# Thirteen FFN evictions, three result copies and two casts of v move from VectorE to ScalarE, and the PSUM banks are dealt out anew

## The chip, the core and the metric

The kernel runs on one core of a Trainium2 chip. The core has five engines, each with its own instruction queue, worked off strictly in order: TensorE (PE) multiplies matrices into PSUM, VectorE (DVE) and ScalarE (ACT) read PSUM and SBUF, GpSimd (POOL) works on SBUF, and SyncE (SP) issues DMAs. The engines wait for each other through semaphores. PSUM has eight banks of 128 partitions by 512 float32 values. The metric is the device time of one execution in microseconds (us), the lower the better. The three runs of the kernel before gave 174.99, 175.62 and 176.35 us, a median of 175.62.

## The reference

Windowed attention with a few global positions, and behind it a feed-forward network (FFN) with a maximum over three products:

```python
scores = scale * np.matmul(q, k.transpose(0, 1, 3, 2))        # 4 batches, 8 heads, 768 x 768, 64 wide
is_global = pos[None, :] < 8
is_local = (rel >= 0) & (rel < 96)
scores = scores + bias                                        # -slope of the head * distance
scores = np.where(is_global | is_local, scores, -1e9)
a = exp(scores - max) / sum
attn = np.matmul(a, v)                                        # to x: 3072 tokens x 512
h = np.maximum(np.maximum(x @ w1, x @ w2), x @ w3)            # 3072 x 768
out = h @ w_out                                               # 3072 x 512, float32
```

## The kernel before

The 3072 tokens are 24 tiles T of 128 (six for each batch). A tile's attention needs its own keys and those of the tile before it, since a query sees 96 positions back, with the 8 global positions copied into rows of the tile before. The FFN takes the tiles in seven chunks c of 4, 2, 2, 4, 4, 4 and 4 tiles (`SIZES`), so a product of a chunk has 512 columns, or 256 in chunks 1 and 2.

The whole order of work is written out by hand in the string `SCHEDULE`. Each word is a unit: a letter, numbers, and behind `@` the slot that the unit's output takes. The order of the words is the order in every engine's queue, and the slot decides who has to wait for whom: a unit that writes a slot waits until all readers of what lay there before are done. The units that matter here:

- `F c.f.j @bank`: PE, four matmuls of input product j (0, 1, 2) of FFN block f (0 to 5) of chunk c into a PSUM bank (line 433).
- `f c.f.j.how @slot`: the eviction of that product. For j = 0 it is a copy into the bf16 buffer h01, by ScalarE if `how` is 0 and by VectorE if it is 1 (line 447). For j = 1 VectorE takes the maximum with h01 in place (line 449), and for j = 2 the maximum into the buffer ht (line 452). There are five h01 slots.
- `O c.tt @bank`: PE, six matmuls of the second product of one tile (line 457); `o c.tt.how @slot` copies its result to SBUF, by ScalarE (0) or VectorE (1) (line 471); `s` issues its DMA to memory from SP (line 477).
- `v T.e.how`: casts half of a v tile to bf16, by ScalarE (0), VectorE (1) or GpSimd (2) (line 254).
- `S`, `e`, `m`, `A`, `n` of a tile: the scores (PE, two banks, line 349), the exponential (ACT, line 356), the mask (DVE, lines 365 and 367), the product with v (PE, two banks, lines 391 and 394), and the reciprocal and division (DVE, lines 402 and 403).
- `t` and `u`, or `Z`: the transposition of the attention's result to xT by PE and a copy, or by a DMA of SP (line 424). `x`, `y`, or `X`: the same for q and k. `l` loads q, k and v, `c` casts q and k (line 195, or 201 on GpSimd).
- `E`: the second product of all four tiles of the last chunk, the last of them in three pieces, with their copies and stores (lines 457, 462 and 463); its banks come from `LAST_BANKS`. One product of chunk 5, `O5.0`, is left behind it.

The index `how` picks the engine in one line:

```python
copies = (nc.scalar.copy, nc.vector.tensor_copy, nc.gpsimd.tensor_copy)
```

Of the kernel before, what the change touches and what calls it, by code (L numbers as in the profile page):

```python
# [611 lines left out]
```

## Time and profile before

| what | value |
|---|---|
| median of three runs | 175.62 us (174.99 to 176.35) |
| the profiled execution's own time | 176.69 us |
| its span, first to last instruction | 174.8 us |
| TensorE busy | 165.9 us, 95% |
| VectorE busy | 131.9 us, 75% |
| ScalarE busy | 95.4 us, 55% |
| GpSimd busy | 54.7 us, 31% |
| granted TensorE clock | 0.996 of full speed |

The profile is one execution on the chip. Busy times of PE are modelled at the ends, since matmuls are pipelined: a 512-column matmul is shown with 0.379 us, while the next one starts 0.216 us after it. So PE's share says little by itself; what it loses is seen in gaps between the starts of matmuls and in the idle time that is written behind a row in brackets, with what ended it. A row of a group reads: line, engine, operation, output<-input, shapes, count, then busy us and mean ns of one, then idle us before these instructions and what ended it. A few records of matmuls are missing.

### The profile page before, as it was taken

To read this page: it belongs to the slowest core of one execution; us is meant where nothing else is said; L and a number is where in the kernel's file an instruction comes from. 1 tells how busy PE (TensorE), PEld (TensorE's weight loads), DVE (VectorE), ACT (ScalarE), POOL (GpSimd) and SP (SyncE) were. 2 spreads that over 40 slices of the span, in tenths; PEclk is the share of its full clock that TensorE was granted. 3 is DMA by queue.
4 is the path that set the end of the run, shared out by engine and by line. 5 is a ranking of instruction groups with operands and counts; after the bars stand their busy time and mean duration, and the time that the engine had idled before them with its cause. 6 is when DMAs were issued, how large, how long until landed. Compare 5 with 4: busy or idle time off the path is not lost.

```text
span 174.8 us, 3865 instructions
## 1 busy us (share of the span) xinstructions
PE 165.9 (95%) x1485; PEld 93.6 (54%) x1507; DVE 131.9 (75%) x268; ACT 95.4 (55%) x147; POOL 54.7 (31%) x99
## 2 busy tenths in 40 slices
PE   7997999999999999898999999999999999999991
PEld 2555745577676877544445545544445554444460
DVE  7889864988599897989898678899578993074910
ACT  5988897672868788440667688200345651402051
POOL 4049295057586717003730003240530000000000
PEclk9999999999999999999999999999999999999998
DMA  5999999999899899999996759998990046370035
GB/s 149 352 292 327 402 360 385 270 371 311 229 303 179 139 183 266 267 290 284 165 135 112 114 145 306 305 210 260 231 213 20 0 120 137 121 286 4 0 119 185
DMA packets 66403, 37.36 MB, mean 214 GB/s; under 512 B 24144, under 2 KB 61392, under 8 KB 66384
## 3 DMA queue, kind: packets, MB, share of 16 engines
q1 hardware_dynamic: 66240, 37.04, 83.3%
q8 instruction: 12, 0.20, 0.5%
q10 hardware_dynamic: 144, 0.07, 0.1%
q14 instruction: 7, 0.06, 0.1%
HBM read 25.17 MB, written 6.29 MB: 180 GB/s over the span
## 4 chain that ended last, share of the span: by engine, by line
PE 76%; DVE 10%; DMA 6%; ACT 3%; issue 2%; SPq 0%; DVEq 0%
PE psum L433 44%; PE psum L457 17%; PE psum L349 6%; DMA xT<-xb 3%; DMA rawqk<-in_k_dram 3%; DVE P L365 3%; PE psum L391 3%; PE psum L394 2%; PE psum L276 2%; DVE ht L452 1%; DVE xb L403 1%; ACT P L356 1%; PE psum L270 1%; DVE qb L195 1%; PE psum L335 1%
## 5 line engine op out<-in xcount | busy, mean ns | idle before, releaser
L433 PE MATMUL psum<-xT,w 128*128 128x512 bf16 (+1 forms) x491 | 97.5, 348 | 1.5 <-DMA xT<-xb 0.7
L433 PEld LDWEIGHTS <-w 128*128 128x128 bf16 x504 | 47.6, 98 | 42.9 <-DMA xT<-xb 0.9
L356 ACT ACTIVATE P<-psum 128x1024 bf16<-128x1024 f32 (+1 forms) x48 | 43.3, 954 | 10.4 <-PE psum L349 10.3
L449 DVE TENSOR_TENSOR h<-h,psum 128x512 bf16<-128x512 bf16 (+1 forms) x42 | 25.0, 605 | 15.9 <-PE psum L433 12.4
L457 PE MATMUL psum<-wo,ht 128*128 128x512 bf16 (+2 forms) x147 | 33.4, 362 | 0.5
L447 ACT CAST h<-psum 128x512 bf16<-128x512 f32 (+1 forms) x27 | 13.8, 523 | 33.1 <-PE psum L433 29.8
L452 DVE TENSOR_TENSOR ht<-h,psum 128x512 bf16<-128x512 bf16 (+1 forms) x42 | 26.2, 644 | 2.1 <-PE psum L433 0.9
L365 DVE TENSOR_TENSOR P<-P,wmask 128x1024 bf16<-128x1024 bf16 x34 | 25.2, 752 | 2.0 <-ACT P L356 1.7
L457 PEld LDWEIGHTS <-ht 128*128 128x128 bf16 x156 | 13.8, 98 | 13.5 <-DVE ht L452 0.2
L254 POOL CAST va<-rawv 64x512 bf16<-64x512 f32 x28 | 18.5, 668 | 4.8 <-DMA rawv<-in_v_dram 3.7
L323 POOL COPY va<-vaf 4x260 int32<-4x260 int32 x17 | 7.2, 424 | 34.9 <-PE psum L394 34.5
L403 DVE TENSOR_TENSOR xb<-psum,rz 128x512 bf16<-128x512 f32 x24 | 16.6, 692 | 0.8
L201 POOL CAST qb<-rawk 128x512 bf16<-128x512 f32 x12 | 7.5, 654 | 23.7 <-DMA rawk<-in_k_dram 23.7
L349 PE MATMUL psum<-qkT 64*128 64x128 bf16 x352 | 14.4, 217 | 0.5 <-DVE qkT L315 0.4
L391 PEld LDWEIGHTS <-P 128*128 128x128 bf16 x192 | 12.6, 97 | 3.2 <-ACT P L356 0.4
L349 PEld LDWEIGHTS <-qkT 64*128 64x128 bf16 x352 | 10.0, 94 | 7.9 <-issue 5.9
L391 PE MATMUL psum<-va,P 128*128 128x65 bf16 x160 | 12.7, 193 | 0.7 <-DVE ht L452 0.6
L447 DVE CAST h<-psum 128x512 bf16<-128x512 f32 (+1 forms) x15 | 9.1, 615 | 5.1 <-PE psum L433 5.1
L471 ACT COPY staging<-psum 128x512 f32<-128x512 f32 x14 | 8.2, 592 | 8.8 <-PE psum L457 8.8
L201 POOL CAST qb<-rawq 128x512 bf16<-128x512 f32 x14 | 8.9, 664 | 9.0 <-DMA rawq<-in_q_dram 5.0
L394 PEld LDWEIGHTS <-P 128*128 128x128 bf16 x160 | 10.5, 97 | 2.1 <-issue 0.7
L394 PE MATMUL psum<-va,P 128*128 128x65 bf16 x128 | 9.9, 193 | 0.0
(72 smaller groups left out, 120.6 us busy)
## 6 DMA issues: line engine op xcount, KB each, us to landing
rawv<-in_v_dram SPq DMA_DIRECT2D x12, 512.0 KB, 7.0
out_dram<-staging SPq DMA_DIRECT2D x21, 256.0 KB, 2.7
rawq<-in_q_dram SPq DMA_DIRECT2D x10, 512.0 KB, 7.1
rawk<-in_k_dram SPq DMA_DIRECT2D x10, 512.0 KB, 7.3
staging<-in_moe_w_dram SPq DMA_DIRECT2D x3, 1024.0 KB, 9.3
staging<-in_moe_w_dram SPq DMA_DIRECT2D x3, 512.0 KB, 8.8
staging<-in_moe_w_out_dram SPq DMA_DIRECT2D x3, 512.0 KB, 6.3
out_dram<-staging SPq DMA_DIRECT2D x5, 128.0 KB, 2.2
```

The costliest lines, as they stand in the source:

```text
L254: copies[how](heads(va(T))[64 * e:64 * e + 64, :, 0:D], src)
L349: nc.tensor.matmul(sp[:, hh, j2, ds], qT(T - ds, 1, hsl, jp), qT(T, 0, hsl, jp), start=not how, stop=True, skip_group_check=True)
L356: nc.scalar.activation(P[:, :, 0:n], sps[T, g].rearrange("p a b d n -> p (a b) d n")[:, :, 0:n], AF.Exp, bias=0.0, scale=scale)
L365: mul(P, P, wmask[:, g, :, 0:2])
L391: nc.tensor.matmul(o, P[:, i, 0], heads(va(T))[:, h], start=True, stop=(t == 0), skip_group_check=True)
L394: nc.tensor.matmul(o, P[:, i, 1], heads(va(T - 1))[:, h], start=False, stop=True, skip_group_check=True)
L403: nc.vector.tensor_tensor(out=x.rearrange("p (g h) d -> p g h d", g=2), in0=o4[:, :, :, 0:64], in1=rz[:, :, :, None].to_broadcast([128, 2, ...
L433: nc.tensor.matmul(ps, w123[f // 2][:, j, dm, (f % 2) * 128:(f % 2) * 128 + 128], xT[c][:, dm], start=(dm == 0), stop=(dm == 3))
L447: copies[how](h01, ps)
L449: nc.vector.tensor_max(h01s[c, f], h01s[c, f], ps)
L452: nc.vector.tensor_max(dst, h01s[c, f].rearrange("p (t e i) -> p t e i", e=2, i=64), ps.rearrange("p (t e i) -> p t e i", e=2, i=64))
L457: nc.tensor.matmul(po, ht[c][:, f, tt * 128:(tt + 1) * 128], wo[:, f, cols], start=(f == 0), stop=(f == NF - 1))
```

## The change

Only the two strings of numbers change: the order of the units stays word for word. Eighteen units get another engine, VectorE (1) before and ScalarE (0) after:

- `f` with j = 0 of (chunk.block) 0.4, 1.2, 1.5, 2.5, 3.0, 3.1, 4.1, 4.0, 5.2, 5.1, 6.2, 6.4 and 6.5;
- `o` 0.1, 2.0 and 4.0;
- `v` 17.1 and 17.0.

ScalarE runs each at the place that the word has in the common order. Beside that, 99 units that write PSUM get other banks, nearly all of them `F`, `O`, `S`, `A` and `t`, and `LAST_BANKS` is dealt anew. The diff, cut to some of its lines:

```diff
-    e3.1@7 V2.1.2 n0@1 t0@2 W0.0.2 c1.2.2.1 u0.0@0 x2.1.2@3 y2.1.2.0@2 w1.2@2 x2.0.2@2 A3@4 t1@6 u1.0 n2@2
+    e3.1@7 V2.1.2 n0@1 t0@2 W0.0.2 c1.2.2.1 u0.0@0 x2.1.2@3 y2.1.2.0@2 w1.2@2 x2.0.2@4 A3@6 t1@2 u1.0 n2@2
...
-    F1.5.0@3 m7.0.1 v8.1.2 F1.5.1@4 A7@6 f1.5.0.1@0 m6.1.1 m6.0.1 o0.2.0@0 y4.1.2.0@0 f1.5.1.1 f1.5.2.1
-    x4.0.2@3 y4.0.2.0 G7.0 l0.6.2@1 c0.6.2.2 F1.4.2@5 O0.1@4 f1.4.2.1 n7@2 o0.1.1@1 A6@0 l2.5.2@2 S8.1.0@2
+    F1.5.0@3 m7.0.1 v8.1.2 F1.5.1@4 A7@6 f1.5.0.0@0 m6.1.1 m6.0.1 o0.2.0@0 y4.1.2.0@0 f1.5.1.1 f1.5.2.1
+    x4.0.2@3 y4.0.2.0 G7.0 l0.6.2@1 c0.6.2.2 F1.4.2@1 O0.1@2 f1.4.2.1 n7@2 o0.1.0@1 A6@0 l2.5.2@2 S8.1.0@4
...
-    F3.4.0@2 F3.0.0@1 f3.4.0.0@4 f3.0.0.1@0 m13.0.1 v13.1.1 f2.4.2.1 F3.1.0@4 F3.3.0@5 c0.9.2.0@2 f3.3.0.0@1
-    A12@2 n12@1 f2.3.2.1 f3.1.0.1@2 F3.1.1@1 f3.1.1.1 v13.0.1 l1.9.2@0 c1.9.2.1 F3.0.2@0 F3.0.1@5 f3.0.1.1
-    F3.1.2@4 f3.0.2.1@1 F3.2.0@1 F3.2.2@2 l1.7.2@6 c1.7.2.2 f3.1.2.1 F3.5.0@3 A13@4 V13.1.1 f3.5.0.1@3 n13@0
+    F3.4.0@2 F3.0.0@1 f3.4.0.0@4 f3.0.0.0@0 m13.0.1 v13.1.1 f2.4.2.1 F3.1.0@4 F3.3.0@1 c0.9.2.0@2 f3.3.0.0@1
+    A12@2 n12@1 f2.3.2.1 f3.1.0.0@2 F3.1.1@0 f3.1.1.1 v13.0.1 l1.9.2@0 c1.9.2.1 F3.0.2@1 F3.0.1@2 f3.0.1.1
+    F3.1.2@0 f3.0.2.1@1 F3.2.0@3 F3.2.2@2 l1.7.2@6 c1.7.2.2 f3.1.2.1 F3.5.0@0 A13@4 V13.1.1 f3.5.0.1@3 n13@0
...
-    V16.0.2 m19.0.1 l0.10.2@3 F4.0.1@0 F4.1.1@7 m19.1.1 f4.4.0.0@1 F4.5.2@6 c0.10.2.2@2 A19@2 Z16 n19@1 Z19
-    G19.0 s0.1 V19.0.2 s2.1 f4.1.1.1 f4.1.2.1@0 V19.1.1 F4.0.0@4 F4.4.1@5 A17@2 c1.10.2.0 f4.0.0.1@3 n17@2
-    F4.5.1@7 f4.5.1.1 F4.2.1@1 F4.3.2@4 f4.5.2.1 f4.4.1.1 F4.0.2@2 F4.3.1@3 F4.4.2@5 f4.2.1.1 v22.1.1
-    f4.0.1.1 f4.3.1.1 f4.0.2.1 f4.3.2.1 F4.2.2@1 Z17 F5.1.1@0 F5.2.0@3 F5.5.0@2 s1.1 F5.3.0@4 F5.0.0@6
+    V16.0.2 m19.0.1 l0.10.2@3 F4.0.1@0 F4.1.1@2 m19.1.1 f4.4.0.0@1 F4.5.2@3 c0.10.2.2@2 A19@4 Z16 n19@1 Z19
+    G19.0 s0.1 V19.0.2 s2.1 f4.1.1.1 f4.1.2.1@0 V19.1.1 F4.0.0@6 F4.4.1@7 A17@4 c1.10.2.0 f4.0.0.0@3 n17@2
+    F4.5.1@2 f4.5.1.1 F4.2.1@1 F4.3.2@6 f4.5.2.1 f4.4.1.1 F4.0.2@2 F4.3.1@3 F4.4.2@7 f4.2.1.1 v22.1.1
+    f4.0.1.1 f4.3.1.1 f4.0.2.1 f4.3.2.1 F4.2.2@0 Z17 F5.1.1@1 F5.2.0@6 F5.5.0@2 s1.1 F5.3.0@3 F5.0.0@4
...
-    F6.4.0@4 F6.2.0@7 f6.0.0.0@2 f6.0.1.1 F6.4.1@2 f6.0.2.1@0 F6.3.1@5 o4.2.0@6 f6.2.0.1@3 F6.3.0@3
-    f6.4.0.1@0 F6.1.1@4 f6.4.1.1 f6.4.2.1 s4.3 s4.0 f6.3.0.0@4 F6.3.2@1 F6.1.0@2 s5.2 F6.2.1@3 s4.2 s5.1
-    s4.1 f6.1.0.0@1 s3.0 s5.3.2 f6.3.1.1 f6.1.1.1 f6.3.2.1 f6.2.1.1 F6.2.2@2 f6.2.2.1 f6.1.2.1 F6.5.1@4
-    F6.5.0@1 f6.5.0.1@2 F6.5.2@5 f6.5.1.1 f6.5.2.1 E@7 O5.0@2 o5.0.0@5 s5.0.2
+    F6.4.0@2 F6.2.0@7 f6.0.0.0@2 f6.0.1.1 F6.4.1@3 f6.0.2.1@0 F6.3.1@5 o4.2.0@6 f6.2.0.0@3 F6.3.0@4
+    f6.4.0.0@0 F6.1.1@2 f6.4.1.1 f6.4.2.1 s4.3 s4.0 f6.3.0.0@4 F6.3.2@1 F6.1.0@3 s5.2 F6.2.1@4 s4.2 s5.1
+    s4.1 f6.1.0.0@1 s3.0 s5.3.2 f6.3.1.1 f6.1.1.1 f6.3.2.1 f6.2.1.1 F6.2.2@3 f6.2.2.1 f6.1.2.1 F6.5.1@2
+    F6.5.0@1 f6.5.0.0@2 F6.5.2@3 f6.5.1.1 f6.5.2.1 E@7 O5.0@2 o5.0.0@5 s5.0.2
...
-LAST_BANKS = (6, 7, 3, 0, 1, 4, 5, 2)
+LAST_BANKS = (6, 7, 5, 4, 0, 1, 3, 2)
```

More of the change, by code (lines that the diff above doesn't have):

```diff
@@ L83 @@
-    F6.4.0@4 F6.2.0@7 f6.0.0.0@2 f6.0.1.1 F6.4.1@2 f6.0.2.1@0 F6.3.1@5 o4.2.0@6 f6.2.0.1@3 F6.3.0@3
-    f6.4.0.1@0 F6.1.1@4 f6.4.1.1 f6.4.2.1 s4.3 s4.0 f6.3.0.0@4 F6.3.2@1 F6.1.0@2 s5.2 F6.2.1@3 s4.2 s5.1
-    s4.1 f6.1.0.0@1 s3.0 s5.3.2 f6.3.1.1 f6.1.1.1 f6.3.2.1 f6.2.1.1 F6.2.2@2 f6.2.2.1 f6.1.2.1 F6.5.1@4
-    F6.5.0@1 f6.5.0.1@2 F6.5.2@5 f6.5.1.1 f6.5.2.1 E@7 O5.0@2 o5.0.0@5 s5.0.2
+    f4.3.0.0@0 v20.0.2 G18.0 F4.1.2@1 f4.1.0.0@3 c0.11.2.2@1 m17.0.1 v17.0.0 l2.11.2@2 n16@3 s3.1 f4.5.0.0@4
@@ new lines @@
+    v23.0.2 F5.0.1@4 v21.0.2 f5.1.0.0@2 f5.1.1.1 s2.0 X20@2 S20.0.0@0 v22.0.1 S20.1.0@6 f5.0.1.1 G20.2
+    f5.5.0.0@1 e20.0@3 e20.1@4 F5.5.1@2 f5.5.1.1 F5.2.2@4 v20.1.2 f5.3.1.1 F5.2.1@5 m20.1.1 F5.4.0@0
+    f5.2.1.1 m20.0.1 f5.2.2.1@1 F5.1.2@1 f5.1.2.1 X21 f5.4.0.0@0 s3.3 X23@3 s0.3 S21.1.0@2 S21.0.0@6 e21.0@2
+    F5.0.2@4 X22 f5.0.2.1 v23.1.2 e21.1@6 s0.2 A20@0 F5.4.1@5 V20.0.1 m21.0.1 F5.4.2@4 G21.1 S22.1.0@2
+    S22.0.0@6 G22.0 e22.1@1 f5.4.1.1 e22.0@7 m21.1.1 f5.4.2.1 V20.1.1 n20@0 O4.0@5 m22.1.1 F5.3.2@4 f5.3.2.1
```

50 lines of the change are left out of this document (22 added, 28 removed).

## The prediction

> **What bounds the kernel now.** First the page: the busy shares and the chain that ended last.
>
> ```profile
> PE 165.9 (95%) x1485; PEld 93.6 (54%) x1507; DVE 131.9 (75%) x268; ACT 95.4 (55%) x147; POOL 54.7 (31%) x99
> PE 76%; DVE 10%; DMA 6%; ACT 3%; issue 2%; SPq 0%; DVEq 0%
> ```
>
> TensorE holds three quarters of the chain, VectorE a tenth, ScalarE 3%. There are 1485 matmuls beside 1507 weight loads, so 22 records are missing, and counts of matmuls below can be one short. Whether PE really runs without a hole is seen in the chain in order of time (start, length, what), near the end:
>
> ```profile
> 155.42 9.23 PE psum L433 x42
> ...
> 164.65 1.51 PE psum L457 x7
> ```
>
> 9.23 us for 42 matmuls is 0.220 us each, about 0.216 without the modelled tail of the first, so an F unit (four matmuls of 512 columns) takes 0.86 us, and the stretch is solid. A change of the other engines can then give back only what PE loses in waits, and costs whatever waits it adds. The order of time (start, length, what, and in brackets the idle time ahead of it) shows two larger ones behind the 25th us:
>
> ```profile
> 72.81 1.04 PE L433 MATMUL psum<-xT,w 128*128 128x512 bf16 x3 [0.66 <-DMA xT<-xb]
> 83.12 0.19 PE L391 MATMUL psum<-va,P 128*128 128x65 bf16 x1 [0.59 <-DVE ht L452]
> ```
>
> The first waits for a transfer, which no moved eviction feeds. The second, A13, waits until VectorE's f3.1.2 has left bank 4: that one the change can reach. The rest, by the gaps between matmul starts, are at most 0.3 us apiece.
>
> **The change part by part.** *Durations.* The same operation on both engines, from the groups by shape:
>
> ```profile
> L447 ACT CAST h<-psum 128x512 bf16<-128x512 f32 x19 | 10.9, 585 | 28.1 <-PE psum L433 24.8 <-DVE ht L452 3.1
> L447 DVE CAST h<-psum 128x512 bf16<-128x512 f32 x11 | 7.5, 686 | 4.9 <-PE psum L433 4.8
> L471 ACT COPY staging<-psum 128x512 f32<-128x512 f32 x14 | 8.2, 592 | 8.8 <-PE psum L457 8.8
> L471 DVE COPY staging<-psum 128x512 f32<-128x512 f32 x6 | 4.1, 684 | 0.2 <-PE psum L457 0.2
> L254 ACT CAST va<-rawv 64x512 bf16<-64x512 f32 x4 | 2.5, 618 | 0.0
> L254 DVE CAST va<-rawv 64x512 bf16<-64x512 f32 x8 | 3.4, 423 | 0.1
> ```
>
> Of the 13 FFN evictions 10 have 512 columns and 3 (chunks 1 and 2) have 256. VectorE loses 10 x 0.686 + 3 x 0.684 + 2 x 0.423 = 9.8 us and the three short ones, of its 131.9; ScalarE gets 10 x 0.585 + 3 x 0.592 + 2 x 0.618 = 8.9 us and the three. Neither is a saving by itself: only the places count where PE waits.
>
> *Evictions with cover*, costed at nothing. f0.4.0 goes behind f0.3.0 on ScalarE, but its bank is wanted over a microsecond later. f1.2.0 and f2.5.0 end no later than now. o2.0 and v17.1 run while ScalarE waits for PE. o4.0 ends about three microseconds later than now, still ahead of its bank's next product, and SP's queue, which holds only stores by then, has the time of chunk 6 to catch up. f4.1.0 has the most behind it:
>
> ```profile
> 106.15 1.29 ACT L447 CAST h<-psum 128x512 bf16<-128x512 f32 x2
> ...
> 107.45 1.07 ACT L447 CAST h<-psum 128x512 bf16<-128x512 f32 x2
> ...
> 107.14 3.61 PE L433 MATMUL psum<-xT,w 128*128 128x512 bf16 x16
> ```
>
> f4.1.0 and v17.0 enter behind the first row and ahead of the second (f4.5.0, f4.4.0). f4.1.0 ends near 107.45 + 0.59 = 108.05, f4.5.0 at 109.1, f4.4.0 at 109.7. PE's units in the third row start at 107.14 and every 0.86 us: F4.1.1, which takes bank 2 from f4.1.0, at 108.86; F4.5.2, which takes bank 3 from f4.5.0, at 109.73. That leaves 0.6 to 0.8 us. If ScalarE came 1 us later (one more exponential ahead), 0.2 to 0.4 us would be paid.
>
> *f1.5.0 and o0.1.* Here the moved copy has work queued behind it:
>
> ```profile
> 48.39 1.07 ACT L287 COPY qkT<-psum 128x1024 bf16<-128x1024 bf16 x1
> 50.41 1.01 ACT L287 COPY qkT<-psum 128x1024 bf16<-128x1024 bf16 x1 [0.95 <-PE psum L276]
> ...
> 52.90 1.94 ACT L356 ACTIVATE P<-psum 128x1024 bf16<-128x1024 f32 x2 [0.84 <-PE psum L349]
> ```
>
> ```profile
> 49.05 0.42 DVE L447 CAST h<-psum 128x256 bf16<-128x256 f32 x1 [0.26 <-PE psum L433]
> 50.80 0.78 DVE L452 TENSOR_TENSOR ht<-h,psum 128x256 bf16<-128x256 bf16 x2
> 50.21 0.60 PE L433 MATMUL psum<-xT,w 128*128 128x256 bf16 x4
> 50.82 0.81 PE L457 MATMUL psum<-wo,ht 128*128 128x512 bf16 x2
> ```
>
> F1.5.0 is ready at 49.05, so o0.2 (now just ahead of the first row), both qkT copies and a small copy stand behind f1.5.0: the first three end at about 49.95, 50.9 and 51.9, by the lengths shown. F1.4.2 (third row of the second fence) takes o0.2's bank at 50.21, so it is just in time. o0.1 and the copy behind it send the exponentials from 52.90 to about 53.4, and S9 takes their bank some 0.2 us after they leave it. O0.1 (last row) takes the bank of f1.5.2, the first of the pair at 50.80, which ends at 51.24 now and, with VectorE 0.42 us ahead, at 50.8. Value: nothing. Bounds: a gain of 0.1, the difference of o0.1's two durations, which F1.1.2 waits for; a loss of 0.5, should VectorE not be ahead.
>
> *f3.0.0 and f3.1.0*, the stop at 83.12. VectorE's order before it (POOL's cast included):
>
> ```profile
> 74.75 0.69 DVE L447 CAST h<-psum 128x512 bf16<-128x512 f32 x1 [0.74 <-PE psum L433]
> ...
> 76.84 0.20 DVE L402 RECIPROCAL rz<-psum 128x8 f32<-128x8 f32 x1
> ...
> 78.00 0.68 DVE L447 CAST h<-psum 128x512 bf16<-128x512 f32 x1
> ...
> 79.94 1.63 POOL L201 CAST qb<-rawk 128x512 bf16<-128x512 f32 x2 [10.13 <-DMA rawk<-in_k_dram]
> 79.97 1.13 DVE L195 CAST qb<-rawk 128x1024 bf16<-128x1024 f32 x1
> 81.02 0.67 DVE L449 TENSOR_TENSOR h<-h,psum 128x512 bf16<-128x512 bf16 x1
> 81.73 1.33 DVE L452 TENSOR_TENSOR ht<-h,psum 128x512 bf16<-128x512 bf16 x2
> ...
> L195 DVE CAST qb<-rawk 128x1024 bf16<-128x1024 f32 x2 | 1.9, 932 | 0.0
> ```
>
> The 0.69 us won at 74.75 is lost again at 76.84, where the reciprocal waits for A12, which PE ends at 76.7. The 0.76 us at 78.00 stays: f3.1.1 starts near 78.03, the cast at 79.21, ahead of POOL's, which waits for its transfer until 79.94. The group of both casts of this kind has a mean of 932 ns, so the other, with no POOL cast ahead of it, took 0.73. I take 0.74, since POOL isn't ahead here either; 1.13 is the other end. f3.1.2 then ends at 81.91 (82.30) instead of 83.06. But the new slots give that bank to F3.5.0, one unit before A13. F3.5.0, which started at 81.7 (A13's 83.12 less the wait and 0.86), starts at 81.96 (82.35), and A13 follows 0.86 later: 82.82 (83.21) against 83.12. **Gain 0.30 us** (bounds: 0.30 gained, 0.09 lost). (The Trainium skill, "SBUF — State Buffer", Who interferes with whom: a VectorE instruction that takes the port pair it shares with GpSimd and a GpSimd one exclude each other, and whoever issues first holds the pair for its whole length. The trace agrees: VectorE's cast, 0.03 us behind POOL's, took 0.4 us longer. By that rule the cast, issued first, has the short length and the term is 0.30; were POOL first, it would be -0.09.)
>
> *f4.0.0, f5.2.0, f5.1.0.* VectorE runs without a hole from 113.96 to 122.5:
>
> ```profile
> 114.28 0.69 DVE L447 CAST h<-psum 128x512 bf16<-128x512 f32 x1
> 114.89 0.20 DVE L402 RECIPROCAL rz<-psum 128x8 f32<-128x8 f32 x1
> ...
> 118.80 1.28 DVE L449 TENSOR_TENSOR h<-h,psum 128x512 bf16<-128x512 bf16 x2
> 120.00 1.94 DVE L452 TENSOR_TENSOR ht<-h,psum 128x512 bf16<-128x512 bf16 x3
> ```
>
> ```profile
> 113.57 5.77 PE L433 MATMUL psum<-xT,w 128*128 128x512 bf16 x26
> ```
>
> Without f4.0.0 all from 114.89 comes 0.61 us earlier (the distance of the first two starts). PE's units follow from 113.57 every 0.86 us: F4.2.2 is the seventh, at 118.75, F5.2.0 the ninth, at 120.48. Now neither waits. The new slots give F4.2.2 the bank of f4.0.1, whose end moves from 119.49 to 118.88, and F5.2.0 that of f4.3.2, from 121.33 to 120.72. With 0.05 us of signalling F4.2.2 starts at 118.93, F5.2.0 at 120.77. **Loss 0.29 us.** f5.2.0 falls behind f5.0.0 on ScalarE (ends 125.2, wanted at 126.8), f5.1.0 ends at 125.7 as now: nothing.
>
> *Chunk 6.* f6.2.0 and f6.4.0 end 0.1 to 0.2 us earlier than now. f6.5.0 ends at 164.4 instead of 164.9, but PE is busy with the last products until about 166.65, when f6.5.2 is needed, and it is there at 166.45 already:
>
> ```profile
> 162.99 1.34 DVE L452 TENSOR_TENSOR ht<-h,psum 128x512 bf16<-128x512 bf16 x2
> 164.22 0.67 DVE L447 CAST h<-psum 128x512 bf16<-128x512 f32 x1
> 164.93 0.69 DVE L449 TENSOR_TENSOR h<-h,psum 128x512 bf16<-128x512 bf16 x1
> 165.72 0.73 DVE L452 TENSOR_TENSOR ht<-h,psum 128x512 bf16<-128x512 bf16 x1
> ```
>
> The slots cost here: F6.5.2 starts at 163.62 (164.49, where the last products start, less 0.86) and now takes bank 3 from f6.2.2, the first of the two in the first row, which ends at 163.72; it starts at 163.77. **Loss 0.15 us**, with nothing behind it to hide it. The last product's banks (5 and 4 in place of 3 and 0) are free long before.
>
> *Sum.* -0.30 + 0.29 + 0.15 = +0.14 us on the profiled execution's 176.69: 176.83. Scaled to the median of the three runs, 175.62, that is **175.8**. Terms from -0.4 to +0.9 by the bounds above.
>
> **The rivals.** *The slots are handed over before VectorE is ahead* (slower). In the trace as it stands, the new owners of four banks would wait: O0.1 0.47 us (bank left at 51.24, wanted at 50.82), A13 0.85 (F3.5.0 at 83.11, A13 at 83.97), F4.2.2 and F5.2.0 0.90 together, F6.5.2 0.15. If ScalarE's copies end no earlier than VectorE's did, so that its maxima wait for them, the sum is 2.37 us: 178.0 on the median. The point from which it decides is 0.6 us of delay in a ScalarE copy. Against it: ScalarE stands idle at f3.1.0, f4.0.0 and f6.5.0. Chance 0.16. (The Trainium skill, "ScalarE: Activation LUTs", Rules for kernel authors, gives plain elementwise work to VectorE, up to about 3x faster in bf16. By an estimate from that page's factor a copy would hold ScalarE for 3 x 0.686 = 2.06 us, f4.1.0 would end at 109.5, and this rival would come true. The rows above speak against it for copies out of PSUM, 585 ns against 686, so it adds no chance.)
>
> *VectorE's lead goes further than I carry it* (faster): the A13 stop goes whole (0.59), as do the small ones at O0.1, F1.1.2, F3.4.1 and A19 (0.1 to 0.3 us each, some 0.7 together), and no new wait comes: 174.4. Over 1% would need the transfer's 0.66 too: 173.7. Against it: the owners change one unit earlier, as at F3.5.0. Chance 0.12, of it 0.04 for the larger.
>
> *The edit doesn't reach the engines*: the last number of an f, o or v unit indexes the three copies directly, so this is under 0.01, with no gain or loss.
>
> **How the numbers follow.** Forecast 0.71, slower rival 0.16, faster rival 0.12, rest 0.01. About 1% (1.75 us) is what a measurement of this kernel can tell from no change; the three runs alone span 0.8%. Over 1% faster: 0.04; slower: 0.16 less 0.01 for the part of that case that stays below; the remaining 0.81 is within. Range: downwards to the faster rival less some spread, 174.5; upwards half the slower rival with the same spread, 177.6.
>
> **What the profile of the changed kernel would show.** Right: PE's matmuls of A13 begin 0.2 to 0.4 us earlier relative to F3.4.0, with a short wait now ahead of F3.5.0; a stop of about 0.2 us at F4.2.2; VectorE near 121 us busy, ScalarE near 105. Wrong: "DVE h L449 <- ACT h L447" growing from 3.0 us by more than 2; PE waiting for ScalarE's L447 anywhere; or the wait for the xT transfer changing by more than 0.5 us, which I leave as it is.

## The result, and the profile after

The changed kernel takes 176.75 us, the median of 19 runs (175.82 to 177.72). The kernel before, beside it on the same chip, takes 175.89 us, the median of 19 runs (174.99 to 176.48). The ratio is **1.0041, with an interval of 1.0026 to 1.0057**: slower by about 0.7 us (the two medians lie 0.86 apart), which is less than the 1% that the prediction set as its bound. The forecast had been +0.14 us. The profiled execution of the changed kernel took 177.72 us with a span of 175.6 us, against 176.69 and 174.8 before, so in the two profiles the difference is 0.8 us of span; each of these two executions lies 0.8 to 1.0 us above the median of its kernel.

First the busy times and the chain from the page of the changed kernel:

```profile
PE 166.8 (95%) x1507; PEld 93.3 (53%) x1507; DVE 122.5 (70%) x250; ACT 104.1 (59%) x165; POOL 53.9 (31%) x99
PE 82%; DVE 6%; DMA 3%; ACT 3%; POOL 2%; issue 2%; SPq 0%; DVEq 0%; ACTq 0%
```

The edit reached the engines: VectorE lost 18 instructions and 9.4 us, ScalarE got 18 and 8.7 us. PE's share of the chain rose from 76% to 82% and VectorE's fell from 10% to 6%. The kernel is more purely bound by PE than before, and still slower.

The groups by shape of the changed kernel (busy us, mean ns of one, idle time before and what ended it) show the same prices as before: 0.587 us for an eviction by ScalarE, 0.593 for a result's copy, 0.618 for the cast of half a v tile.

```profile
L447 ACT CAST h<-psum 128x512 bf16<-128x512 f32 x29 | 16.1, 587 | 28.9 <-PE psum L433 22.5 <-DVE ht L452 6.4
L471 ACT COPY staging<-psum 128x512 f32<-128x512 f32 x17 | 9.7, 593 | 8.7 <-PE psum L457 8.7
L254 ACT CAST va<-rawv 64x512 bf16<-64x512 f32 x6 | 3.7, 618 | 0.1
```

Where the 0.8 us came from is seen by laying the starts of PE's units in the two profiles side by side. The table is worked out from the starts of the matmuls; "shift" is the start after less the start before, and a step in it is a wait that came or went.

| unit | shift, us | what happened there |
|---|---|---|
| O0.1 | +0.44 | a new wait of 0.34 for the eviction f1.5.2; 0.10 was there before it |
| F3.4.0 | -0.41 | the wait of before for an xT transfer is gone |
| A13 | -0.80 | its stop is gone; F3.5.0 waits 0.16 instead |
| F4.4.0 | +0.22 | a new wait of about 1.0 for an xT transfer |
| F4.4.1 | +0.37 | A19, ahead of it, waits longer for its masks |
| F4.2.2 | +0.52 | a new wait of 0.15 for f4.0.1 |
| F5.2.0 | +0.63 | a new wait of 0.12 for f4.3.2 |
| F6.5.2 | +0.76 | a new wait of 0.15 for f6.2.2 |
| the end | +0.76 | |

Two of these steps are large enough for the changed kernel's view in order of time to mark them on PE (start, length, what, and in brackets the idle time ahead and what ended it). The second row is the place where the stop at A13 was:

```profile
51.25 1.02 PE L457 MATMUL psum<-wo,ht 128*128 128x512 bf16 x4 [0.34 <-DVE ht L452]
...
82.31 0.19 PE L391 MATMUL psum<-va,P 128*128 128x65 bf16 x1
...
102.54 0.81 PE L433 MATMUL psum<-xT,w 128*128 128x512 bf16 x3 [1.04 <-DVE va L325]
```

O0.1 waits for VectorE's f1.5.2, A13 follows without a bracket, and F4.4.0 waits 1.04 us. PE was ready for it at about 101.4. The bracket names VectorE at line 325, a copy that ends at 102.47. But by the trace the last transposing transfer into chunk 4's xT landed at 102.45, against 101.80 in the profile before, and it is this that F4.4.0 waits for: in seven of the fourteen profiles of this case F4.4.0 starts 0.09 us after that landing, and in the version with the early masks (below) it starts at 102.73 while the copy of line 325 ends at 103.19.

The table of waits by engine tells the rest of the trade. These rows are of the changed kernel, with the total us, the number and the longest:

```profile
PE psum L433 <- DVE va L325: 1.0, 1, 1.0
PE psum L457 <- DVE ht L452: 0.3, 1, 0.3
DVE h L449 <- ACT h L447: 9.6, 5, 4.1
```

VectorE now waits 9.6 us for ScalarE's copies instead of 3.0, and PE waits for ScalarE's copies nowhere. VectorE's waits of this kind lie where it had time to spare: a run below has 9.2 us of them and the time of the kernel before.

### The profile page after: what moved, and what is told of

The parts are those of the page before. It is cut to its first block, busy times and chain, and to the rows that moved or that the text cites. A ratio compares the mean times of both kernels' runs of the same rounds, so it can differ in the third digit from the quotient of the medians.

```text
span 175.6 us, 3888 instructions
## 1 busy us (share of the span) xinstructions
PE 166.8 (95%) x1507; PEld 93.3 (53%) x1507; DVE 122.5 (70%) x250; ACT 104.1 (59%) x165; POOL 53.9 (31%) x99
## 4 chain that ended last, share of the span: by engine, by line
PE 82%; DVE 6%; DMA 3%; ACT 3%; POOL 2%; issue 2%; SPq 0%; DVEq 0%; ACTq 0%
PE psum L433 51%; PE psum L457 17%; PE psum L349 5%; PE psum L391 3%; DMA rawqk<-in_k_dram 3%; DVE P L365 3%; PE psum L394 3%; ACT P L356 2%; PE psum L335 1%; DVE xb L403 1%; POOL va L254 1%; PE psum L270 1%; PE psum L418 1%; POOL va L323 1%; PE psum L276 1%
## 5 line engine op out<-in xcount | busy, mean ns | idle before, releaser
L433 PE MATMUL psum<-xT,w 128*128 128x512 bf16 (+1 forms) x504 | 99.2, 349 | 1.1 <-DVE va L325 1.0
L447 ACT CAST h<-psum 128x512 bf16<-128x512 f32 (+1 forms) x40 | 20.1, 529 | 34.2 <-PE psum L433 27.7
L457 PE MATMUL psum<-wo,ht 128*128 128x512 bf16 (+2 forms) x156 | 33.9, 363 | 0.3 <-DVE ht L452 0.3
L365 DVE TENSOR_TENSOR P<-P,wmask 128x1024 bf16<-128x1024 bf16 x34 | 25.7, 768 | 4.4 <-ACT P L356 4.3
L471 ACT COPY staging<-psum 128x512 f32<-128x512 f32 x17 | 9.7, 593 | 8.7 <-PE psum L457 8.7
L201 POOL CAST qb<-rawk 128x512 bf16<-128x512 f32 x12 | 7.0, 616 | 21.9 <-DMA rawk<-in_k_dram 21.8
L402 DVE RECIPROCAL rz<-psum 128x8 f32<-128x8 f32 x24 | 4.9, 203 | 8.7 <-PE psum L394 4.7
```

The lines of the kernel that those rows point to most:

```text
L365: mul(P, P, wmask[:, g, :, 0:2])
L433: nc.tensor.matmul(ps, w123[f // 2][:, j, dm, (f % 2) * 128:(f % 2) * 128 + 128], xT[c][:, dm], start=(dm == 0), stop=(dm == 3))
L447: copies[how](h01, ps)
L457: nc.tensor.matmul(po, ht[c][:, f, tt * 128:(tt + 1) * 128], wo[:, f, cols], start=(f == 0), stop=(f == NF - 1))
```

## The experiments

All ratios are against the kernel before, run beside each on the same chip. That kernel's medians there were 175.90 to 176.07 us.

### One half at a time

*ScalarE copies on the old banks.* The 18 units get their new engine, and every bank stays as before. The diff is against the kernel before, and the other 17 units follow the same pattern:

```diff
-    F0.2.0@5 f0.4.0.1@1 F0.1.0@6 v4.1.2 v4.0.2 l2.3.2@0 f0.1.0.0@2 q2@0 v5.1.0 F0.0.0@0 F0.5.1@1 F0.4.1@4
+    F0.2.0@5 f0.4.0.0@1 F0.1.0@6 v4.1.2 v4.0.2 l2.3.2@0 f0.1.0.0@2 q2@0 v5.1.0 F0.0.0@0 F0.5.1@1 F0.4.1@4
...
```

> The 18 units run on ScalarE as in the changed kernel, every PSUM bank is that of the kernel before. Theory (the lost time comes from the new banks, and time won at A13 is lost again at the xT transfers of chunk 4, where F4.4.0 waits): no wait at F4.2.2, F5.2.0 and F6.5.2, 0.39 us less than the changed kernel, a ratio to before of 0.998 to 1.002. Rival (the lost time comes from ScalarE's copies, which end late or stand ahead of other work, and the banks don't matter): ratio about 1.004, as the whole change.

Measured: 176.81 us, ratio 1.0041 (1.0015 to 1.0067). In the order of time of this kernel:

```profile
25.13 1.08 ACT L447 CAST h<-psum 128x512 bf16<-128x512 f32 x2
...
26.26 1.67 PE L433 MATMUL psum<-xT,w 128*128 128x512 bf16 x7 [1.05 <-ACT h L447]
```

The old banks give F0.1.0 the bank of f0.4.0. On VectorE that copy was early; on ScalarE it is the second of the pair in the first row and ends at 26.21, and PE stands still for 1.05 us. In the changed kernel F0.1.0 has bank 3 and does not wait. So the number that came out is that of the rival theory, but the reason is a bank that I had overlooked. The run does not tell what the other 17 copies cost, so a further one left this one copy where it was.

*Seventeen ScalarE copies on the old banks*, with f0.4.0 on VectorE. Against the kernel before, the line above stays as it was, and the first of the 17 edits is:

```diff
-    f1.0.1.1 f1.2.0.1@0 Q0.2 f1.0.2.1@1 x3.1.2@6 y3.1.2.1@3 F0.4.2@5 f0.4.2.1 l1.4.2@3 v6.0.2 Q1.2 F1.1.0@0
+    f1.0.1.1 f1.2.0.0@0 Q0.2 f1.0.2.1@1 x3.1.2@6 y3.1.2.1@3 F0.4.2@5 f0.4.2.1 l1.4.2@3 v6.0.2 Q1.2 F1.1.0@0
...
```

> Old banks, ScalarE for 17 of the 18 units: f0.4.0 stays on VectorE, since with the old banks F0.1.0 waits 1.2 us for it on ScalarE. Theory (ScalarE's copies cost nothing, the banks do): ratio 0.996 to 1.001, A13's wait gone, no wait of PE for a ScalarE copy. Rival (ScalarE's copies cost by themselves): ratio about 1.004, as with all 18.

Measured: 175.74 us, ratio 0.9991 (0.9969 to 1.0013). The copies by themselves cost nothing that can be measured, and gain nothing either. Against the changed kernel's 1.0041 the difference is 0.0050, about 0.9 us, and the two intervals stand apart. With the copies in place it is the banks that make the kernel slower.

*The new banks on the old engines.* Against the kernel before, only the numbers behind `@` and `LAST_BANKS` change, as in the change:

```diff
-    f4.0.1.1 f4.3.1.1 f4.0.2.1 f4.3.2.1 F4.2.2@1 Z17 F5.1.1@0 F5.2.0@3 F5.5.0@2 s1.1 F5.3.0@4 F5.0.0@6
+    f4.0.1.1 f4.3.1.1 f4.0.2.1 f4.3.2.1 F4.2.2@0 Z17 F5.1.1@1 F5.2.0@6 F5.5.0@2 s1.1 F5.3.0@3 F5.0.0@4
...
```

> The new banks, with all 18 units still on VectorE. Theory: the new owners wait for VectorE, F4.2.2 and F5.2.0 together 0.9 us, F6.5.2 0.15 us, A13 begins 0.85 us later than before, which is paid at F4.4.0 as far as PE then comes behind the transfers: 1.0 to 2.4 us in all, ratio 1.006 to 1.013. Rival (the banks don't matter): ratio 0.998 to 1.002.

Measured: 178.13 us, ratio 1.011 (1.008 to 1.014). The order of time on PE of this kernel:

```profile
81.77 1.02 PE L433 MATMUL psum<-xT,w 128*128 128x512 bf16 x4 [0.22 <-DVE h L449]
83.13 1.02 PE L433 MATMUL psum<-xT,w 128*128 128x512 bf16 x4 [0.35 <-DVE ht L452]
...
119.97 2.22 PE L433 MATMUL psum<-xT,w 128*128 128x512 bf16 x9 [0.32 <-DVE h L449]
```

The first two rows are chunk 3's products ahead of A13, the third is F4.2.2. Without VectorE's lead each hand-over of a bank costs PE: by the starts of the matmuls 0.48 us at O0.1, 0.60 at F4.2.2 and F5.2.0 together and 0.15 at F6.5.2, and A13 comes 0.8 to 1.0 us later after F3.4.0 than in the two profiles of before. This is the mechanism of the slower rival by itself. The prediction had priced it at 2.37 us; measured are 2.2 by the medians and 1.9 by the ratio. In the changed kernel the lead takes most of it away again, and what is left over is the loss.

### The last hand-overs

*Five banks back.* In this and the diffs below the first side is the changed kernel. Five units of chunks 4 to 6 get banks whose last reader is earlier:

```diff
-    f4.0.1.1 f4.3.1.1 f4.0.2.1 f4.3.2.1 F4.2.2@0 Z17 F5.1.1@1 F5.2.0@6 F5.5.0@2 s1.1 F5.3.0@3 F5.0.0@4
-    f4.2.2.1 f5.3.0.0@4 f5.0.0.0@3 v21.1.2 F5.1.0@0 s0.0 l1.11.2@0 F5.3.1@3 c1.11.2.2 f5.2.0.0@0 f4.4.2.1
+    f4.0.1.1 f4.3.1.1 f4.0.2.1 f4.3.2.1 F4.2.2@1 Z17 F5.1.1@0 F5.2.0@5 F5.5.0@2 s1.1 F5.3.0@3 F5.0.0@4
+    f4.2.2.1 f5.3.0.0@4 f5.0.0.0@3 v21.1.2 F5.1.0@1 s0.0 l1.11.2@0 F5.3.1@3 c1.11.2.2 f5.2.0.0@0 f4.4.2.1
...
-    F6.5.0@1 f6.5.0.0@2 F6.5.2@3 f6.5.1.1 f6.5.2.1 E@7 O5.0@2 o5.0.0@5 s5.0.2
+    F6.5.0@1 f6.5.0.0@2 F6.5.2@5 f6.5.1.1 f6.5.2.1 E@7 O5.0@2 o5.0.0@5 s5.0.2
```

> The changed kernel with five banks dealt otherwise: F4.2.2 on 1, F5.1.1 on 0, F5.1.0 on 1, F5.2.0 on 5, F6.5.2 on 5, all of which are free in time in its trace. Theory: the waits of 0.15, 0.11 and 0.13 us at F4.2.2, F5.2.0 and F6.5.2 go, 0.39 us less than the changed kernel, ratio to before 1.001 to 1.003. Rival (ScalarE's copies): the waits turn up elsewhere and the ratio stays 1.004.

Measured: 176.27 us, ratio 1.0013 (0.9992 to 1.0034). How the three waits went is seen from PE's pace between chunk 4 and the second products of the last chunk. First the kernel before in a second profile (F4.5.1, then the first product of `E`), then the changed kernel, then this one:

```profile
112.56 2.11 PE L433 MATMUL psum<-xT,w 128*128 128x512 bf16 x9
...
163.50 2.97 PE L457 MATMUL psum<-wo,ht 128*128 128x512 bf16 x12
```

```profile
113.94 0.59 PE L433 MATMUL psum<-xT,w 128*128 128x512 bf16 x2
...
165.24 1.03 PE L457 MATMUL psum<-wo,ht 128*128 128x512 bf16 x4
```

```profile
113.29 1.46 PE L433 MATMUL psum<-xT,w 128*128 128x512 bf16 x6
...
164.19 2.32 PE L457 MATMUL psum<-wo,ht 128*128 128x512 bf16 x10
```

The stretch lasts 50.94 us before, 51.30 changed, 50.90 with the five banks back: the three small waits are 0.4 us, and these five banks are the whole of them. The medians moved by 0.48 us, which is of the same size, but the intervals of the two ratios overlap, so it is the profile that shows this, not the times.

### What hangs on the execution, and what on the kernel

The waits for xT transfers change between executions, so both kernels were profiled a second time, unchanged.

> The kernel before, profiled a second time. If the waits at F3.4.0 (0.66 us), F4.4.0 and A19 belong to single executions, because they hang on when transfers land, they differ here by some tenths of a microsecond in size from the first profile; if they belong to the order of work they stay within 0.1 us. The ratio is 1.000 and its interval says how fine these comparisons are.

> The changed kernel, profiled a second time. Theory (bank waits and O0.1 belong to the order of work): F4.2.2 0.15, F5.2.0 0.11, F6.5.2 0.13 and O0.1 0.35 us again within 0.05 us, while the 1.1 us at F4.4.0 of the first profile is of that execution and shrinks to some 0.1 to 0.4 us. Rival (the transfers of chunk 4 are made late by the change): F4.4.0 waits about 1 us again. Ratio 1.003 to 1.005 in both cases.

Measured: before 176.06 us (0.9997, 0.9976 to 1.0017), changed 176.56 us (1.0039, 1.0018 to 1.0061). PE in the second profile of the changed kernel, at O0.1 and at F4.4.0:

```profile
51.45 0.81 PE L457 MATMUL psum<-wo,ht 128*128 128x512 bf16 x2 [0.52 <-DVE ht L452]
...
101.97 1.47 PE L433 MATMUL psum<-xT,w 128*128 128x512 bf16 x6
```

and in the second profile of the kernel before, at A13:

```profile
82.21 0.19 PE L391 MATMUL psum<-va,P 128*128 128x65 bf16 x1 [0.46 <-DVE ht L452]
```

The 1.04 us at F4.4.0 is not there the second time, so it is not in every execution of the changed kernel. It isn't peculiar to one execution either: the profiles of three later kernels have brackets of 0.50 to 0.74 us at the same place, each ending 0.09 us after the landing of the last transfer. The 0.8 us at F3.4.0 in the first profile of before doesn't come back either: its transfer landed at 71.73 us instead of 72.77. What recurs is the wait at O0.1 (0.52, more than the 0.35 that was expected), the missing stop at A13, and the waits at F4.2.2, F5.2.0 and F6.5.2 (0.15, 0.12 and 0.15). Between the two second profiles the end of PE's work differs by 0.93 us: +0.51 at O0.1, -0.25 at A13, +0.29 at F3.4.1, +0.27 at F4.2.2 and F5.2.0 together, +0.15 at F6.5.2, which is 0.97. The +0.29 at F3.4.1 is not in the first pair of profiles. PE and VectorE in the second profile of the changed kernel show where it comes from:

```profile
86.84 1.02 PE L433 MATMUL psum<-xT,w 128*128 128x512 bf16 x4 [0.24 <-DVE ht L452]
```

```profile
83.22 0.66 DVE L325 COPY va<-vaf 4x520 bf16<-4x520 bf16 x1 [1.64 <-PE psum L394]
```

F3.4.1 waits for the maximum f3.2.2, and in VectorE's queue ahead of that stands this copy from SBUF to SBUF. It took 0.66 us where a pair of GpSimd's casts had started 0.10 us ahead of it (at 83.12), and 0.29 in the first profile of the changed kernel, where GpSimd's casts started at 83.50, behind its end. The difference of 0.37 covers the wait. So, as far as these two profiles show, it too hangs on what VectorE's instruction meets on GpSimd, and on the execution.

*The transfer ahead of F4.4.0 taken off the DMA queues.* Tile 14's transposition goes to PE and ScalarE, on top of the five banks: `Z14` goes, and `t14`, `u14` come in its place, further ahead. That adds four transposing matmuls to PE. The words move along the lines; the two new places are:

```diff
-    o3.0.1@9 e16.0@2 V15.1.2 A18@0 e16.1@6 n18@0 o3.2.1@10 m16.1.1 X17 O3.1@7 G16.0 Z14 o3.1.0@11 m16.0.1
...
+    O2.1@7 v18.0.0 o2.1.0@7 m15.0.1 S18.0.0@0 S18.1.0@2 X19 Z13@1 V14.0.1 O3.3@6 t14@4 m15.1.1 e18.0@3
+    e18.1@4 X16@1 u14.0 o3.3.0@8 A15@0 n15@2 O3.0@7 S19.1.0@0 v17.1.0 m18.0.1 S16.1.0@2 m18.1.1 e19.1@1
```

> As the one with five banks, and tile 14's xT comes from four PE transposes (0.22 us of PE) and a ScalarE copy instead of a transposing DMA, so that SP issues nine of them in place of ten between 81 and 101 us. Theory (F4.4.0 waits for the last of these transfers, which land at 102.45 us): they land about 1.9 us earlier, F4.4.0 no longer waits, and PE, 0.9 us ahead by A13 and the rest, keeps that less 0.22: 0.7 us less than with five banks alone, ratio to before 0.996 to 0.999. Rival (the wait at F4.4.0 isn't the transfers'): 0.2 us more than with five banks alone.

Measured: 176.03 us, ratio 0.9991 (0.9968 to 1.0014), against 1.0013 (0.9992 to 1.0034) without it. F4.4.0 shows no wait in this profile:

```profile
102.53 1.68 PE L433 MATMUL psum<-xT,w 128*128 128x512 bf16 x7
```

The run doesn't test the wait well: PE had waited 0.5 us for another transfer ahead of F3.4.0 and came to F4.4.0 later than with the five banks alone (102.53 against 101.86). The intervals overlap, so that this wait costs the changed kernel anything in the median is not shown.

### The wait at O0.1

In the prediction f1.5.2 was to end 0.42 us earlier once VectorE is rid of f1.5.0. VectorE and GpSimd in the changed kernel, in order of time:

```profile
48.81 1.58 DVE L367 TENSOR_TENSOR P<-P,wmask 128x512 bf16<-128x512 bf16 x2
50.31 0.41 DVE L449 TENSOR_TENSOR h<-h,psum 128x256 bf16<-128x256 bf16 x1
50.76 0.78 DVE L452 TENSOR_TENSOR ht<-h,psum 128x256 bf16<-128x256 bf16 x2
```

```profile
48.40 1.72 POOL L201 CAST qb<-rawq 128x512 bf16<-128x512 f32 x2 [1.96 <-DMA rawq<-in_q_dram]
```

and VectorE in the second profile of the kernel before:

```profile
49.45 1.04 DVE L367 TENSOR_TENSOR P<-P,wmask 128x512 bf16<-128x512 bf16 x2
```

The two masks of tile 6 start at 48.81 instead of 49.45, and run into GpSimd's pair of casts from 48.40 to 50.12. The two together take 1.58 us in place of 1.04 (by the trace up to 0.83 us for one, where a mask of this size alone takes 0.42). What VectorE gained, it lost there, and the maxima start at 50.31 and 50.76 (50.36 and 50.80 before). The other half of the wait is the new bank. With the new banks and f1.5.0 still on VectorE (the run above) the masks take 1.04 us and O0.1 waits all the same, since nothing has put VectorE ahead. VectorE and PE there:

```profile
49.54 1.04 DVE L367 TENSOR_TENSOR P<-P,wmask 128x512 bf16<-128x512 bf16 x2
...
51.45 1.46 PE L457 MATMUL psum<-wo,ht 128*128 128x512 bf16 x6 [0.48 <-DVE ht L452]
```

So the new bank asks for 0.48 us of lead, and the masks must be the reason why the lead isn't there. If they are, then on the old bank, which VectorE's line 449 frees one maximum sooner, O0.1 must wait where the masks are long and not where they are short. With f1.5.0 back on VectorE, which holds the masks back, they should be short.

*f1.5.0 back on VectorE*, in the changed kernel with the 13 banks from F1.4.2 to A9 as before:

```diff
-    F1.5.0@3 m7.0.1 v8.1.2 F1.5.1@4 A7@6 f1.5.0.0@0 m6.1.1 m6.0.1 o0.2.0@0 y4.1.2.0@0 f1.5.1.1 f1.5.2.1
-    x4.0.2@3 y4.0.2.0 G7.0 l0.6.2@1 c0.6.2.2 F1.4.2@1 O0.1@2 f1.4.2.1 n7@2 o0.1.0@1 A6@0 l2.5.2@2 S8.1.0@4
+    F1.5.0@3 m7.0.1 v8.1.2 F1.5.1@4 A7@6 f1.5.0.1@0 m6.1.1 m6.0.1 o0.2.0@0 y4.1.2.0@0 f1.5.1.1 f1.5.2.1
+    x4.0.2@3 y4.0.2.0 G7.0 l0.6.2@1 c0.6.2.2 F1.4.2@5 O0.1@4 f1.4.2.1 n7@2 o0.1.0@1 A6@0 l2.5.2@2 S8.1.0@2
...
```

> The changed kernel with f1.5.0 back on VectorE and the 13 banks of F1.4.2 to A9 as in the kernel before. Theory (with f1.5.0 gone, VectorE's masks of tile 6 start earlier and run into a GpSimd cast, so that the time won there is lost and O0.1 waits): the two masks take 0.71 and 0.41 us instead of 0.83 each, O0.1's wait of 0.35 to 0.5 us goes, the ratio to before falls from 1.004 to about 1.002. Rival (the masks are long for another reason): they stay at 0.83 us.

Measured: 176.48 us, ratio 1.0026 (1.0007 to 1.0044). VectorE and PE in this kernel:

```profile
49.24 0.42 DVE L447 CAST h<-psum 128x256 bf16<-128x256 f32 x1 [0.26 <-PE psum L433]
49.58 1.04 DVE L367 TENSOR_TENSOR P<-P,wmask 128x512 bf16<-128x512 bf16 x2
...
51.01 1.24 PE L457 MATMUL psum<-wo,ht 128*128 128x512 bf16 x5
```

The masks take 1.04 us again, and O0.1, the last row, has no bracket. The wait is gone, as the theory asks. That it did not go by the 13 banks alone, which were changed in the same kernel, is told by the 17 copies on the old banks: there these banks are as before, f1.5.0 is on ScalarE, and the masks and O0.1 look like this:

```profile
49.38 1.57 DVE L367 TENSOR_TENSOR P<-P,wmask 128x512 bf16<-128x512 bf16 x2
```

```profile
51.34 1.02 PE L457 MATMUL psum<-wo,ht 128*128 128x512 bf16 x3 [0.28 <-DVE h L449]
```

The median of the run with f1.5.0 back is 0.27 us below the changed kernel's, and the intervals overlap.

### A version that beats both

*Banks of both places as before, and the masks of tile 19 early.* On top of the five banks, the 13 banks go back, f1.5.0 stays on ScalarE, and the two masks of tile 19 move ahead of tile 16's reciprocal, into the time in which VectorE waits 2.22 us for A16 in the changed kernel:

```diff
-    f4.3.0.0@0 v20.0.2 G18.0 F4.1.2@1 f4.1.0.0@3 c0.11.2.2@1 m17.0.1 v17.0.0 l2.11.2@2 n16@3 s3.1 f4.5.0.0@4
-    V16.0.2 m19.0.1 l0.10.2@3 F4.0.1@0 F4.1.1@2 m19.1.1 f4.4.0.0@1 F4.5.2@3 c0.10.2.2@2 A19@4 Z16 n19@1 Z19
+    f4.3.0.0@0 v20.0.2 G18.0 F4.1.2@1 f4.1.0.0@3 c0.11.2.2@1 m17.0.1 m19.0.1 m19.1.1 v17.0.0 l2.11.2@2 n16@3
+    s3.1 f4.5.0.0@4 V16.0.2 l0.10.2@3 F4.0.1@0 F4.1.1@2 f4.4.0.0@1 F4.5.2@3 c0.10.2.2@2 A19@4 Z16 n19@1 Z19
...
```

> The changed kernel with the five banks dealt otherwise, the 13 banks of F1.4.2 to A9 as in the kernel before (O0.1 takes the bank of f1.5.1 and not of f1.5.2), and the masks of tile 19 put ahead of tile 16's division on VectorE, into the 2.2 us in which it waits for A16, so that they don't meet GpSimd's casts. Theory: the waits at O0.1 (0.35), F4.2.2, F5.2.0, F6.5.2 (0.39) and A19 (0.3 to 0.5) go; the first may be lost at F3.4.0; 0.7 to 1.2 us less than the changed kernel, ratio to before 0.997 to 1.000. Rival (A19's wait isn't due to the meeting with GpSimd): m19 takes 2 us here too and the ratio stays that of the five banks, 1.0013.

Measured: **175.65 us, ratio 0.9973 (0.9954 to 0.9991)**, faster than the kernel before, though by a quarter of a percent only. VectorE in the changed kernel, and then in this one:

```profile
107.54 0.21 DVE L402 RECIPROCAL rz<-psum 128x8 f32<-128x8 f32 x1 [2.22 <-PE psum L394]
...
108.39 3.02 DVE L365 TENSOR_TENSOR P<-P,wmask 128x1024 bf16<-128x1024 bf16 x2
```

```profile
105.35 1.90 DVE L365 TENSOR_TENSOR P<-P,wmask 128x1024 bf16<-128x1024 bf16 x3 [0.22 <-ACT P L356]
107.73 0.21 DVE L402 RECIPROCAL rz<-psum 128x8 f32<-128x8 f32 x1 [0.48 <-PE psum L394]
```

In the changed kernel the two masks take 3.02 us, with casts of GpSimd on a v and a q tile beside them from 108.35 on; moved into the hole, three masks take 1.90 us, and A19 no longer waits. O0.1 still waits 0.22 us here, now for f1.5.1 on VectorE at line 449, since the masks of tile 6 still collide. In this profile PE also waits for transfers, 0.46 us ahead of tile 14's scores and 0.50 at F4.4.0.

*The same with f1.5.0 back on VectorE,* against the version above:

```diff
-    F1.5.0@3 m7.0.1 v8.1.2 F1.5.1@4 A7@6 f1.5.0.0@0 m6.1.1 m6.0.1 o0.2.0@0 y4.1.2.0@0 f1.5.1.1 f1.5.2.1
+    F1.5.0@3 m7.0.1 v8.1.2 F1.5.1@4 A7@6 f1.5.0.1@0 m6.1.1 m6.0.1 o0.2.0@0 y4.1.2.0@0 f1.5.1.1 f1.5.2.1
```

> As the one with five banks, 13 banks and the masks of tile 19 ahead, with f1.5.0 back on VectorE too. Theory: the 0.2 us that O0.1 still waited there goes, ratio to before 0.995 to 0.998. Rival (it is lost at F3.4.0 or F4.4.0 to the transfers): unchanged at 0.997.

Measured: 176.05 us, ratio 0.9997 (0.9974 to 1.0021). This is above both expectations. O0.1 waits 0.18 us in this profile, and the second mask met a GpSimd cast all the same (0.43 and 0.87 us by the trace). So on the old bank it is the meeting of masks and casts that decides, not f1.5.0 itself: where they miss each other the wait is gone, where they meet it is there, and the start of the casts hangs on a transfer. The intervals of this run and the one before overlap, so f1.5.0's place gives nothing sure in the median.

*Only engines and masks,* against the kernel before: its banks, 16 copies on ScalarE (f0.4.0 and f1.5.0 not), and the early masks:

```diff
-    f4.3.0.0@0 v20.0.2 G18.0 F4.1.2@1 f4.1.0.1@3 c0.11.2.2@1 m17.0.1 v17.0.1 l2.11.2@2 n16@3 s3.1 f4.5.0.0@4
+    f4.3.0.0@0 v20.0.2 G18.0 F4.1.2@1 f4.1.0.0@3 c0.11.2.2@1 m17.0.1 m19.0.1 m19.1.1 v17.0.0 l2.11.2@2 n16@3
...
```

> Old banks; ScalarE for 16 of the 18 units (f0.4.0 and f1.5.0 stay on VectorE); the masks of tile 19 ahead of tile 16's division. Theory (the engine moves are good where VectorE's lead is used, and the new banks aren't needed for it): no wait at O0.1 and A19, A13's wait gone whole, ratio to before 0.994 to 0.998. Rival (the new banks are needed for the gain): above 0.999.

Measured: 176.01 us, ratio 0.9981 (0.9962 to 1.0000). Its profiled execution has the wait for a transfer at F4.4.0, under the label "issue" and of 0.65 us. The ratio falls between the theory (up to 0.998) and the rival (above 0.999). Its interval overlaps that of the version above, so what the remaining new banks are worth is not shown.

*The version that beats both, with tile 14 transposed by PE,* by the edit already shown for `t14` and `u14`:

```diff
-    o3.0.1@9 e16.0@2 V15.1.2 A18@0 e16.1@6 n18@0 o3.2.1@10 m16.1.1 X17 O3.1@7 G16.0 Z14 o3.1.0@11 m16.0.1
...
```

> The five banks, the 13 banks of F1.4.2 to A9, the masks of tile 19 ahead, and tile 14's xT by PE transposes instead of a transposing DMA. Theory (what PE wins ahead of chunk 4 is lost at F4.4.0 to the last of the transfers): no wait at F4.4.0, ratio to before 0.994 to 0.997, below the 0.997 without it. Rival (the 0.22 us of PE transposes cost as much as the transfers did): 0.997 to 0.999.

Measured: 175.41 us, ratio 0.9971 (0.9953 to 0.9989). F4.4.0 starts without a wait, and the stretch from F4.5.1 to `E` lasts 50.90 us:

```profile
101.52 1.68 PE L433 MATMUL psum<-xT,w 128*128 128x512 bf16 x7
...
112.48 2.11 PE L433 MATMUL psum<-xT,w 128*128 128x512 bf16 x9
...
163.38 3.19 PE L457 MATMUL psum<-wo,ht 128*128 128x512 bf16 x13
```

It too is faster than the kernel before, and against 0.9973 without the edit it is no difference that these runs can tell; the ratio lies on the border of the two expectations.

This profile also has the clearest case of the masks. f1.5.0 is on ScalarE, the banks around O0.1 are the old ones, and here GpSimd's casts came later. VectorE, GpSimd and PE:

```profile
48.86 0.75 DVE L367 TENSOR_TENSOR P<-P,wmask 128x512 bf16<-128x512 bf16 x2
```

```profile
49.17 1.47 POOL L201 CAST qb<-rawq 128x512 bf16<-128x512 f32 x2 [2.19 <-DMA rawq<-in_q_dram]
```

```profile
50.80 1.46 PE L457 MATMUL psum<-wo,ht 128*128 128x512 bf16 x5
```

The two masks take 0.75 us together, the maxima at line 452 begin at 50.16 instead of 50.76, and O0.1 does not wait. Up to this place the order, the engines and the banks are those of the run in which O0.1 waited 0.22 us; what differs is the start of the casts.

## Why the prediction was right or wrong, step by step

**The bound: right.** PE's waits decide. VectorE lost 9.4 us of work and the time did not fall.

**The covered evictions at nothing: right, but for one bank.** In the changed kernel PE waits for ScalarE's line 447 nowhere, and 17 copies on the old banks give 0.9991. What the step did not say is that f0.4.0 needs its new bank: with the old one, PE loses 1.05 us at F0.1.0.

**A13, -0.30: right in mechanism, and in size within 0.1.** It measured -0.39 in the first pair of profiles (-0.80 less the -0.41 that was there already at F3.4.0) and -0.25 in the second. On the old banks the 17 copies bring A13 0.41 us nearer to F3.4.0 than in the second profile of before (9.75 against 10.16), on the new ones 0.25 (9.91): the 0.15 between them is what the bank of F3.5.0 takes back, as the step said. The choice between 0.74 and 1.13 us for the cast came out as chosen. VectorE around it, in the changed kernel:

```profile
78.73 0.69 DVE L195 CAST qb<-rawk 128x1024 bf16<-128x1024 f32 x1
79.34 0.68 DVE L449 TENSOR_TENSOR h<-h,psum 128x512 bf16<-128x512 bf16 x1
80.06 1.34 DVE L452 TENSOR_TENSOR ht<-h,psum 128x512 bf16<-128x512 bf16 x2
```

The cast takes 0.69 us now that no cast of GpSimd is ahead of it. The short wait that was to appear ahead of F3.5.0 is there, 0.16 us.

**F4.2.2 and F5.2.0, +0.29: right**, 0.27 in both pairs. **F6.5.2, +0.15: right**, 0.15 in both. The rows of VectorE that release these banks came as worked out:

```profile
118.52 1.28 DVE L449 TENSOR_TENSOR h<-h,psum 128x512 bf16<-128x512 bf16 x2
119.73 1.94 DVE L452 TENSOR_TENSOR ht<-h,psum 128x512 bf16<-128x512 bf16 x3
...
163.60 1.34 DVE L452 TENSOR_TENSOR ht<-h,psum 128x512 bf16<-128x512 bf16 x2
```

f4.0.1, the first of the first row, ends at 119.21, and F4.2.2 follows at about 119.27, 0.15 behind PE's pace.

**f1.5.0 and o0.1, 0: the step that failed.** It cost 0.34 us in the first profile and 0.51 in the second, the other end of the bound that was given (0.5, "should VectorE not be ahead"). That f1.5.0 itself would not be late on ScalarE was right; the maxima behind it on VectorE came no earlier (50.76 against 50.80). The failure is that the 0.42 us of the removed copy were carried forward unchanged through two masks, though the very next step looked at what GpSimd does beside a cast. The warning was in the trace of before. The groups by shape of before and of the changed kernel have line 367 as:

```profile
L367 DVE TENSOR_TENSOR P<-P,wmask 128x512 bf16<-128x512 bf16 x7 | 3.3, 505 | 0.2 <-ACT P L356 0.2
```

```profile
L367 DVE TENSOR_TENSOR P<-P,wmask 128x512 bf16<-128x512 bf16 x7 | 3.9, 585 | 0.2 <-ACT P L356 0.2
```

Half of these masks take 0.42 us, and a mean of 0.505 says that some already met GpSimd; the first mask of tile 6 did, with 0.71 us in the trace. The changed kernel pushed it and the next one further into it, 0.83 us each. (The Trainium skill, "SBUF — State Buffer", Who interferes with whom: a VectorE instruction that reads both inputs from SBUF contends with a GpSimd instruction that reads SBUF. The trace agrees: the masks, with both inputs in SBUF, doubled beside the casts, 0.83 us against 0.42.)

**The wait for the xT transfer, left as it is: wrong for the profile, open for the median.** The wait at F3.4.0 was not a property of the kernel: in the second profile of before it is absent. In its place the changed kernel's first profile waits about a microsecond for another transfer, at F4.4.0, and the second profile doesn't. Over all fourteen profiles F4.4.0 starts right behind the landing in seven, after waits of 0.07 to 1.1 us, and without a wait in the others. PE gets to chunk 4 earlier or later by less than a microsecond, and transfers land within a similar spread, so a gain made ahead of this place may or may not pass it.

**The sum.** The terms by the second pair of profiles are +0.51, -0.25, +0.29, +0.27 and +0.15, together +0.97 against a forecast of +0.14; the ratio over all runs says +0.7. Most of the miss is the one term at O0.1; the +0.29 at F3.4.1 was not foreseen, and it is in one of the two executions only. The three terms that were forecast make +0.03 and +0.17 us in the two pairs, which is close to +0.14; the rest is what the prediction put at nothing. The measured 176.75 us lies inside the range of 174.5 to 177.6 because the range was wide, not because the sum was complete.

**The rivals.** The slower one is what the banks do alone: 2.2 us by the medians (1.9 by the ratio), 2.37 worked out. It did not come true for the whole change, because ScalarE's copies give VectorE its lead nearly everywhere; of its four places O0.1 paid all, F4.2.2 with F5.2.0 a third, F6.5.2 the whole, A13 nothing but the 0.15 ahead of F3.5.0. The faster one did not come: VectorE's lead ended at the masks, and the owners of the banks change one unit earlier.

**The signs.** VectorE at 122.5 us busy was expected near 121, ScalarE at 104.1 near 105. The sign "VectorE's line 449 waiting for ScalarE's line 447 grows by more than 2 us" fired (3.0 to 9.6), but was a bad sign: with 17 copies on the old banks, where the time is that of before, the same row stands at 9.2:

```profile
DVE h L449 <- ACT h L447: 9.2, 5, 3.7
```

VectorE has time there. The sign on the xT transfer fired too (the 0.66 us at F3.4.0 went, 1.04 came at F4.4.0), and told of the execution as much as of the change. A13 came 0.40 and 0.25 us earlier after F3.4.0, with 0.2 to 0.4 expected. The sign that counts is a bracket on PE.
